# A chunk's token operands made from kept tokens inside the first unit, and the gate's iterations moved seven steps on

## The chip, the cores and the metric

One Trainium2 chip, one core. The metric is the device time of one execution, in microseconds; of repeated runs the median is given.

## The reference

Linear attention by random features, then a mixture of experts over all 2304 tokens (4 batches of 576, 8 heads of 64, so 512 columns; 8 experts of 1024 hidden columns). All inputs and outputs are float32.

```python
q_p, k_p = phi(q_s), phi(k_s)            # exp(x@omega.T - |x|^2/2 - max) / sqrt(128)
num = einsum('bhsm,bhmd->bhsd', q_p, einsum('bhsm,bhsd->bhmd', k_p, v))
den = einsum('bhsm,bhm->bhs', q_p, sum(k_p, 2)) + 1e-6
x = (num / den) as [2304, 512]
P = exp(x @ w_gate - max)                # [2304, 8]
for _ in range(8):
    P /= P.sum(1, keepdims=True) + 1e-9
    P /= P.sum(0, keepdims=True) + 1e-9
    P *= N / E
out = sum over e of P[:, e:e+1] * (maximum(x @ w1[e], 0) @ w2[e])
```

## The kernel before

**The attention** (`tick`, about 0 to 152 us) makes the tokens `x` in tiles of 128. Per tick PE makes the projections `pp`, the transpositions `tp`, `qp` of queries, the numerators `np`, and for a finished token tile its transposition `xp`; DVE takes maxima, shifts and quotients (`rd`, `xt`), ACT the exponentials `ex`. ACT's `token_copy` (L597) then puts the transposed tile into `xf`, a chunk of six tiles (768 tokens); there are three chunks. The attention's instructions are pinned in the order in which the code writes them.

**Products in seven.** Each matrix product of the experts is done in 2 by 2 blocks with seven products in place of eight, in the order 1, 5, 6, 3, 7, 2, 4, and each float32 operand as a rounded high part and a low rest, three products of parts. `token_operands` (L102) makes for a chunk its seven token operands: for four of them a total of quarters (L116, POOL, for the last chunk DVE), then the high part, called cast here (L120, ACT), the low (L124, DVE), and a store of both to a DRAM tile `xd` (L126, SP, 768 KB). A string (`plan`) says in which tick each is made. For the last chunk, chunk 2, the first products of the experts are interleaved with the making of its operands. `logits` (L168) makes a chunk's gate logits: products `lp` from `xf`, a copy `lg`, transpositions `gp`, and a sum into `prob`.

**The units.** There are 16, two for each expert (four blocks of 128 hidden columns each). A unit goes over the three chunks, the first one in the order 2, 0, 1, and has nine steps of two token tiles. `first` (L696) makes the products with w1 into the banks `hx` and `hz`; operands of the left side of the second product are made from them on DVE and ACT (`left_operands_a` and `_b`, L735 to L773); `second` (L796) makes the products with w2 into the banks `x` and `z`, which DVE adds to the outputs `out` (L818 in expert 0, with the factor of `prob` at L821 after it). Meanwhile ACT, DVE and POOL split the weights of the next unit (L250, L251, L217). `load_next` loads the next token operand from `xd` into one of four buffers `xs` each time one has been used.

**The gate.** `sinkhorn` (L610) is a generator of some 19 parts: maximum, exponential, and eight iterations of two parts each, with nine small DVE operations and one column product `cp` on PE in an iteration. The step loop takes two parts in each step (L1035), from the first step on. Expert 0 is added up without its factor; at its end, in unit 2, the loop writes a multiply of each output tile by its column of `prob` (L1015).

The units' instructions are put in order by a scheduler, so an instruction need not stand where the loop writes it.

Of the kernel before, what the change touches and what calls it, by code (L numbers as in the profile page):

```python
# [9 lines left out]
F32 = mybir.dt.float32  # L10
# [12 lines left out]
def moe_attention_kernel(  # L23
# [26 lines left out]
    N, DM = out.shape  # L50
    E = w_gate.shape[1]
    FF = w1.shape[2]
    P = 128
    KD = DM // P
# [9 lines left out]
    CT = 6  # L64
    NCH = NT // CT
    CL = CT * P
    HL = CL // 2
# [24 lines left out]
    ORDER = [1, 5, 6, 3, 7, 2, 4]  # L92
# [2 lines left out]

    W2AT = [(5, 2), (6, 0), (6, 3), (7, 0), (7, 3), (8, 0), (8, 3)]
    xdram = {}

    def token_tile():
        return xs.tile([P, 2, 2, HL], F32R, tag="xs", bufs=XSB, name="xs")  # L100

    def token_operands(c, x):  # L102

        def q(r, h):
            h = 1 - h
            return x[:, 2 * r : 2 * r + 2, h * HL : (h + 1) * HL]

        last = c == NCH - 1
        gate_steps = logits(c, x)
        if last:  # L110
            next(gate_steps)

        def total(o, i, s):
            eng = nc.vector if last else nc.gpsimd
            a, b = {5: (q(0, 1), s), 6: (q(1, 1), s), 7: (q(1, 1), q(0, 1)), 4: (q(1, 0), s)}[i]
            eng.tensor_tensor(o, a, b, op=ALU.subtract)  # L116

        def cast(i, o):
            t = token_tile()
            nc.scalar.copy(t[:, 0], o)  # L120
            return t

        def low(i, o, t):
            nc.vector.tensor_tensor(t[:, 1], o, raw(t[:, 0]), op=ALU.subtract)  # L124
            xdram[c, i] = xd.tile([P, 2, 2, HL], F32, name=f"xd{c}_{i}")
            nc.sync.dma_start(out=xdram[c, i], in_=raw(t))  # L126

        if last:
            for i in ORDER:
                n = len(traced)  # L130
                o = {3: q(1, 1), 7: q(0, 1), 2: q(1, 0)}.get(i, q(0, 0))
                if i in (5, 6, 7, 4):
                    total(o, i, o)
                t = cast(i, o)
                low(i, o, t)
                pinned.extend(traced[n:])
                xop[0, c, i] = t
                first(0, c, i, 0)
                first(0, c, i, 1)
                next(gate_steps, None)  # L140
                yield
            return


        if c == 0:
            at = {i: {3: q(1, 1), 7: q(0, 1), 2: q(1, 0)}.get(i, q(0, 0)) for i in ORDER}
            plan = "|c1 |c3 l1.s5|c2 l3|c5 l2.s7| l5.s6|c7 |c6 l7| l6.s4| |c4 | l4|"
        else:
            at = {1: q(0, 0), 3: q(1, 1), 2: q(1, 0)}
            for n, i in enumerate((5, 6, 7, 4)):  # L150
                at[i] = vts[n].rearrange("p h c -> p (h c)")[:, : 2 * HL].rearrange("p (k t) -> p k t", k=2)
            plan = "|s5.c1.c3 s7.l1|c2 l3.s6|c5 l2.s4|c7 l5|c6 l7|c4 l6.l4|"
        tiles = {}
        for n, step in enumerate(plan.split()):
            for part in step.split("|"):
                for what in part.split(".") if part else ():
                    i = int(what[1])
                    if what[0] == "s":
                        total(at[i], i, {5: q(0, 0), 6: at[5], 4: at[6]}.get(i))
                    elif what[0] == "c":  # L160
                        tiles[i] = cast(i, at[i])
                    else:
                        low(i, at[i], tiles.pop(i))
                yield
            next(gate_steps, None)
# [132 lines left out]
                yield  # L298


    sc_cm = tc.tile_pool(name="sc", bufs=1, reuse_waits="tile")
    sc = sc_cm.__enter__()
    rw_cm = tc.tile_pool(name="rw", bufs=1, side="right", reuse_waits="tile")
# [71 lines left out]
    xf = {}  # L375
# [207 lines left out]
    def token_transposes(xt, j, t):  # L583

        c = t // CT
        if c not in xf:
            xf[c] = sc.tile([P, KD, CL], F32, tag="xf", bufs=2, name="xf")
        xps = bank("xp")
        xj = xt[:, j].rearrange("p h d -> p (h d)")
        for kk in range(KD):  # L590
            nc.tensor.transpose(xps[:, kk * P : (kk + 1) * P], xj[:, kk * P : (kk + 1) * P], ident)
        return xps
# [50 lines left out]
    outt = {}  # L643
# [11 lines left out]
    def load_next():  # L655

        while loads:
            u, c, i = loads.pop(0)
            if i in RES:
                if (c, i) not in xres:  # L660
                    xres[c, i] = op_.tile([P, 2, 2, HL], F32R, name=f"xr{c}_{i}")
                    nc.sync.dma_start(out=raw(xres[c, i]), in_=xdram[c, i])
                xop[u, c, i] = xres[c, i]
                continue
            xop[u, c, i] = token_tile()
            nc.sync.dma_start(out=raw(xop[u, c, i]), in_=xdram[c, i])
            return
# [108 lines left out]
            6: (sh[:, 0], sl[:, 0]), 3: (sh[:, 1], sl[:, 1]), 2: (bh[:, 0], bl[:, 0]), 4: (bh[:, 1], bl[:, 1]),  # L776
        })

    acc = {}

    def second(s, i):


        u, n = steps[s]
        key, start = {1: ("x", 1), 6: ("x", 0), 7: ("x", 0), 4: ("x", 0), 5: ("z", 1), 3: ("z", 0), 2: ("z", 0)}[i]
        final = s == len(steps) - 1
        if final and i == 4:

            key, start = "y", 1
        if start:  # L790
            acc[key] = bank(key)
        pb = acc[key][:, HD:] if i in (5, 3) else acc[key][:, :HD]
        start = start or i == 2
        prods = [(a, b, f) for a, b in ((0, 0), (0, 1), (1, 0)) for f in range(2)]
        for j, (a, b, f) in enumerate(prods):
            nc.tensor.matmul(  # L796
                pb, lhsT=ops[s][i][a][:, f], rhs=wt[u, 2, i][b][:, f],
                start=bool(start) and j == 0, stop=j == len(prods) - 1, skip_group_check=True,
            )
        e, fb = units[u]  # L800
        r, col, init = {
            1: (0, 0, 1), 6: (0, 1, 1), 7: (1, 1, 0), 4: (1, 0, 1), 5: (1, 1, 1), 3: (0, 1, 0), 2: (0, 0, 0),
        }[i]
        if i == 3:
            return
        pair = tiles_of(u, n)
        t = pair[r]
        if u == 0 and i == 1:
            for tt in pair:
                outt[tt] = op_.tile([P, DM], F32, name=f"out{tt}")  # L810
        o = outt[t][:, col * HD : (col + 1) * HD]
        if i == 2:
            o, pb = outt[t], acc[key]
        if e == 0:
            if u == 0 and init:
                nc.scalar.copy(o, pb)
            else:
                nc.vector.tensor_tensor(o, pb, o, op=ALU.add)  # L818
            return
        p = prob[:, t, e : e + 1]  # L820
        nc.vector.scalar_tensor_tensor(o, in0=pb, scalar=p, in1=o, op0=ALU.mult, op1=ALU.add)  # L821
        if final and i == 7:
            o = outt[t][:, :HD]
            nc.vector.scalar_tensor_tensor(o, in0=pb, scalar=p, in1=o, op0=ALU.mult, op1=ALU.add)
# [185 lines left out]
    for s, (u, n) in enumerate(steps):  # L1010
        c = n // (CT // 2)
        more = u + 1 < len(units)
        if u == NFB:
            for t in tiles_of(u, n):
                nc.vector.tensor_scalar_mul(outt[t], outt[t], prob[:, t, 0:1])  # L1015
        if more:
            if n == 1:
                stage(u + 1, 1)
            if n == 2:
                split(u + 1, 1, ORDER[0])  # L1020
            if n == 2:
                stage(u + 1, 2)
        for k, i in enumerate(ORDER if s + 1 < len(steps) else [1, 5, 6, 3, 2, 4, 7]):
            second(s, i)
            if more and (n, k) in W2AT:
                split(u + 1, 2, ORDER[W2AT.index((n, k))])
            if k < ((5, 5, 4) if s > 2 else (3, 4, 3))[n % 3] and todo:
                pc = todo.pop(0)
                first(*pc)
                j = ORDER.index(pc[2])  # L1030
                if pc[1] == order(pc[0])[-1] and pc[3] == 1 and pc[0] + 1 < len(units) and j + 1 < len(ORDER):
                    split(pc[0] + 1, 1, ORDER[j + 1])
            if i == 7 and s + 1 < len(steps):
                left_operands_a(s + 1)
            if k in (1, 4):  # L1035
                next(gate, None)
        if s + 1 < len(steps):
            left_operands_b(s + 1)
        if s == NFB * NP - 1:
            for _ in gate:  # L1040
                pass
        if u == len(units) - 1:
            t0, t1 = tiles_of(u, n)
            for t, col in ((t0, 1), (t1, 1), (t0, 0), (t1, 0)):
                store(t, col, nc.scalar if s + 1 == len(steps) and t == t1 else nc.sync)
        ops.pop(s)
# [28 lines left out]
```

## Time and profile before

| | us |
|---|---|
| median of 3 runs | 1586.25 (1585.63 to 1586.45) |
| the profiled execution | 1585.57 |
| its span | 1583.8 |
| PE busy | 1561.0 (99%) |
| DVE busy | 1376.4 (87%) |
| ACT busy | 769.3 (49%) |
| POOL busy | 272.1 (17%) |

The profile is of one execution. Busy times are sums over the span; where an engine waited, and for whom, stands in the timelines (idle time in square brackets, with the one that ended it) and in the chain of waits.

### The profile page before, as it was taken

What the parts mean: (1) busy time and instruction counts of PE and PEld (TensorE: products, weight loads), DVE (VectorE), ACT (ScalarE), POOL (GpSimd) and SP (SyncE); (2) the same over time, 40 slices, a digit from 0 to 9 for tenths busy, and PEclk for the clock granted to TensorE, in tenths of its full rate; (3) what the DMA queues carried; (4) which work ended last, traced back from release to release, by engine and by line L of the source; (5) the groups of instructions that cost most, each with busy time, mean ns of one, the idle gap of its engine ahead of it and who ended that gap; (6) DMA issues with size and microseconds to landing.
All of it is one profiled execution on the core that took longest, in us unless ns stands there. A gap on an engine that the chain in (4) does not pass through costs nothing.

```text
span 1583.8 us, 31347 instructions
## 1 busy us (share of the span) xinstructions
PE 1561.0 (99%) x12337; PEld 1534.9 (97%) x12337; DVE 1376.4 (87%) x2600; ACT 769.3 (49%) x1393; POOL 272.1 (17%) x275
## 2 busy tenths in 40 slices
PE   8998999999999999999999999999999999999998
PEld 7876999999999999999999999999999999999997
DVE  6998998999889888889888888989888888888778
ACT  7987655444444444444444444443343444444332
POOL 4664211111011111102010111111010111110000
PEclk9999999999999999999999999999999999999999
DMA  9645866656656665656566666656566565645562
GB/s 220 144 148 219 341 233 215 226 176 242 216 206 218 226 206 202 224 189 227 202 214 212 218 217 208 222 183 224 194 226 226 207 207 208 239 166 182 198 220 80
DMA packets 105330, 329.79 MB, mean 208 GB/s; under 512 B 14816, under 2 KB 44000, under 8 KB 105184
## 3 DMA queue, kind: packets, MB, share of 16 engines
q1 hardware_dynamic: 104896, 327.53, 61.1%
q8 instruction: 98, 1.61, 0.4%
q14 instruction: 48, 0.39, 0.1%
q10 hardware_dynamic: 288, 0.26, 0.0%
HBM read 306.53 MB, written 21.23 MB: 207 GB/s over the span
## 4 chain that ended last, share of the span: by engine, by line
PE 89%; DVE 7%; ACT 2%; DMA 1%; issue 1%; POOL 1%; SPq 0%; DVEq 0%; ACTq 0%
PE hx L696 24%; PE x L796 24%; PE z L796 19%; PE hz L696 18%; DVE sqs L446 1%; DVE out L821 1%; PE pp L436 1%; DVE xs L124 1%; ACT ex L466 0%; PE np L556 0%; DVE wl L251 0%; DVE bl L735 0%; POOL sq L400 0%; PE qp L532 0%; DMA xs<-xd 0%
## 5 line engine op out<-in xcount | busy, mean ns | idle before, releaser
L696 PE MATMUL hx<-xs,wh 128*128 128x384 f32 x1536 | 369.0, 335 | 2.8 <-DMA xs<-xd 1.4
L821 DVE SCALAR_TENSOR_TENSOR out<-x,prob,out 128x256 f32<-128x256 f32 x503 | 236.0, 477 | 83.5 <-PE x L796 81.7
L696 PE MATMUL hz<-xs,wh 128*128 128x384 f32 x1152 | 285.0, 336 | 0.5 <-DVE bl L735 0.5
L696 PEld LDWEIGHTS hx<-xs,wh 128*128 128x128 f32 x1536 | 266.7, 188 | 4.3 <-ACT xs L120 2.0
L217 POOL TENSOR_TENSOR st<-st 128x512 f32<-128x512 f32 x75 | 120.9, 1612 | 616.6 <-DVE wl L251 612.5
L773 ACT ACTIVATE bh<-hr 128x512 fp32r<-128x512 f32 x144 | 91.1, 633 | 251.4 <-PE x L796 246.0
L696 PEld LDWEIGHTS hz<-xs,wh 128*128 128x128 f32 x1152 | 201.3, 188 | 1.6 <-DVE bl L735 1.1
L696 PE MATMUL hx<-xs,wl 128*128 128x384 f32 x768 | 200.6, 335 | 0.0
L821 DVE SCALAR_TENSOR_TENSOR out<-z,prob,out 128x256 f32<-128x256 f32 x252 | 153.3, 609 | 15.5 <-PE z L796 15.1
L250 ACT CAST wh<-st 128x512 fp32r<-128x512 f32 x172 | 103.4, 620 | 107.9 <-PE hx L696 53.9
L770 DVE TENSOR_TENSOR sl<-sm,sh 128x512 fp32r<-128x512 f32 x144 | 117.1, 813 | 41.5 <-ACT sh L769 33.9
L696 PE MATMUL hz<-xs,wl 128*128 128x384 f32 x576 | 152.5, 335 | 0.0
L769 ACT CAST sh<-sm 128x512 fp32r<-128x512 f32 x144 | 89.5, 621 | 102.7 <-PE z L796 80.2
L696 PEld LDWEIGHTS hx<-xs,wl 128*128 128x128 f32 x768 | 137.8, 188 | 0.0
L735 DVE SCALAR_TENSOR_TENSOR sm<-hr,sm 128x256 f32<-128x256 f32 x288 | 131.7, 457 | 3.2
L251 DVE TENSOR_TENSOR wl<-st,wh 128x512 fp32r<-128x512 f32 x172 | 123.2, 727 | 8.9 <-ACT wh L250 8.9
L756 ACT CAST sh<-sm 128x512 fp32r<-128x512 f32 x143 | 89.0, 622 | 67.7 <-PE x L796 64.6
L743 ACT ACTIVATE ah<-hr 128x256 fp32r<-128x256 f32 x144 | 60.2, 418 | 125.8 <-PE x L796 105.1
L796 PE MATMUL z<-wh,sh 128*128 128x256 f32 x576 | 119.0, 281 | 2.3 <-DVE out L821 1.3
L796 PE MATMUL x<-wl,sh 128*128 128x256 f32 x576 | 117.8, 280 | 0.0
L796 PE MATMUL z<-wl,sh 128*128 128x256 f32 x576 | 117.1, 280 | 0.0
L796 PE MATMUL x<-wh,sl 128*128 128x256 f32 x576 | 115.8, 279 | 0.2 <-DVE sl L770 0.2
(161 smaller groups left out, 3405.9 us busy)
## 6 DMA issues: line engine op xcount, KB each, us to landing
xs<-xd SPq DMA_DIRECT2D x329, 768.0 KB, 4.5
st<-in_moe_w_dram SPq DMA_DIRECT2D x64, 512.0 KB, 4.8
xd<-xs SPq DMA_DIRECT2D x21, 768.0 KB, 4.0
v<-in_v_dram SPq DMA_DIRECT2D x8, 512.0 KB, 6.9
q<-in_q_dram SPq DMA_DIRECT2D x8, 512.0 KB, 6.9
out_dram<-out SPq DMA_DIRECT2D x30, 128.0 KB, 2.0
k<-in_k_dram SPq DMA_DIRECT2D x7, 512.0 KB, 7.2
k<-in_k_dram SPq DMA_DIRECT2D x2, 256.0 KB, 3.0
```

What stands on the lines that cost most here:

```text
L217: nc.gpsimd.tensor_tensor(o, a, b, op=op)
L250: nc.scalar.copy(hi, o)
L251: nc.vector.tensor_tensor(lo, o, raw(hi), op=ALU.subtract)
L696: nc.tensor.matmul(pb, lhsT=a[:, k, g * P : (g + 1) * P], rhs=x[:, b, k, :], start=i in (1, 5, 2) and j == 0, stop=j == len(prods) - 1, sk ...
L735: nc.vector.scalar_tensor_tensor(o, in0=a, scalar=0.0, in1=b, op0=ALU.max, op1=op)
L743: nc.scalar.activation(ah, a11, AF.Relu)
L756: nc.scalar.copy(sh, sm)
L769: nc.scalar.copy(sh, sm)
L770: nc.vector.tensor_tensor(sl, sm, raw(sh), op=ALU.subtract)
L773: nc.scalar.activation(bh, a[:, 1:], AF.Relu)
L796: nc.tensor.matmul(pb, lhsT=ops[s][i][a][:, f], rhs=wt[u, 2, i][b][:, f], start=bool(start) and j == 0, stop=j == len(prods) - 1, skip_gro ...
L821: nc.vector.scalar_tensor_tensor(o, in0=pb, scalar=p, in1=o, op0=ALU.mult, op1=ALU.add)
```

## The change

For chunk 1 (`LATE`) no operand is made in the attention: of `token_operands` only its logits are left, and a function `make` that makes one operand (total on POOL, cast, low and store as before) is kept in `late`. `load_next` calls it in unit 0 where it loaded that operand before, so up to four products ahead of use. From unit 1 on, chunk 1's operands are loaded as before. The chunk's tokens stay in a buffer `xl` of its own; `xf` has one buffer in place of two. When `xl` is no longer read, the six output tiles of chunk 1 (`xo`) take its place. The gate's parts are taken from step 7 on.

```diff
--- before.py
+++ after.py
@@ -95,6 +95,8 @@
 
     W2AT = [(5, 2), (6, 0), (6, 3), (7, 0), (7, 3), (8, 0), (8, 3)]
     xdram = {}
+    LATE = NCH - 2
+    late = []
 
     def token_tile():
         return xs.tile([P, 2, 2, HL], F32R, tag="xs", bufs=XSB, name="xs")
@@ -142,14 +144,21 @@
             return
 
 
-        if c == 0:
-            at = {i: {3: q(1, 1), 7: q(0, 1), 2: q(1, 0)}.get(i, q(0, 0)) for i in ORDER}
-            plan = "|c1 |c3 l1.s5|c2 l3|c5 l2.s7| l5.s6|c7 |c6 l7| l6.s4| |c4 | l4|"
-        else:
-            at = {1: q(0, 0), 3: q(1, 1), 2: q(1, 0)}
-            for n, i in enumerate((5, 6, 7, 4)):
-                at[i] = vts[n].rearrange("p h c -> p (h c)")[:, : 2 * HL].rearrange("p (k t) -> p k t", k=2)
-            plan = "|s5.c1.c3 s7.l1|c2 l3.s6|c5 l2.s4|c7 l5|c6 l7|c4 l6.l4|"
+        at = {i: {3: q(1, 1), 7: q(0, 1), 2: q(1, 0)}.get(i, q(0, 0)) for i in ORDER}
+
+        if c == LATE:
+            def make(i):
+                if i in (5, 6, 7, 4):
+                    total(at[i], i, at[i])
+                t = cast(i, at[i])
+                low(i, at[i], t)
+                return t
+
+            late.append(make)
+            yield from gate_steps
+            return
+
+        plan = "|c1 |c3 l1.s5|c2 l3|c5 l2.s7| l5.s6|c7 |c6 l7| l6.s4| |c4 | l4|"
         tiles = {}
         for n, step in enumerate(plan.split()):
             for part in step.split("|"):
@@ -298,6 +307,7 @@
                 yield
 
 
+    xl = ctx.enter_context(tc.tile_pool(name="xl", bufs=1, reuse_waits="tile"))
     sc_cm = tc.tile_pool(name="sc", bufs=1, reuse_waits="tile")
     sc = sc_cm.__enter__()
     rw_cm = tc.tile_pool(name="rw", bufs=1, side="right", reuse_waits="tile")
@@ -584,7 +594,10 @@
 
         c = t // CT
         if c not in xf:
-            xf[c] = sc.tile([P, KD, CL], F32, tag="xf", bufs=2, name="xf")
+            if c == LATE:
+                xf[c] = xl.tile([P, KD, CL], F32, tag="xl", bufs=1, name="xl")
+            else:
+                xf[c] = sc.tile([P, KD, CL], F32, tag="xf", bufs=1, name="xf")
         xps = bank("xp")
         xj = xt[:, j].rearrange("p h d -> p (h d)")
         for kk in range(KD):
@@ -662,6 +675,9 @@
                     nc.sync.dma_start(out=raw(xres[c, i]), in_=xdram[c, i])
                 xop[u, c, i] = xres[c, i]
                 continue
+            if (u, c) == (0, LATE):
+                xop[u, c, i] = late[0](i)
+                return
             xop[u, c, i] = token_tile()
             nc.sync.dma_start(out=raw(xop[u, c, i]), in_=xdram[c, i])
             return
@@ -776,7 +792,7 @@
             6: (sh[:, 0], sl[:, 0]), 3: (sh[:, 1], sl[:, 1]), 2: (bh[:, 0], bl[:, 0]), 4: (bh[:, 1], bl[:, 1]),
         })
 
-    acc = {}
+    acc, late_out = {}, []
 
     def second(s, i):
 
@@ -807,7 +823,12 @@
         t = pair[r]
         if u == 0 and i == 1:
             for tt in pair:
-                outt[tt] = op_.tile([P, DM], F32, name=f"out{tt}")
+                if tt // CT == LATE:
+                    if tt == pair[0] and tt % CT == 0:
+                        late_out.append(xl.tile([P, CT, DM], F32, tag="xl", bufs=1, name="xo"))
+                    outt[tt] = late_out[0][:, tt % CT]
+                else:
+                    outt[tt] = op_.tile([P, DM], F32, name=f"out{tt}")
         o = outt[t][:, col * HD : (col + 1) * HD]
         if i == 2:
             o, pb = outt[t], acc[key]
@@ -1032,7 +1053,7 @@
                     split(pc[0] + 1, 1, ORDER[j + 1])
             if i == 7 and s + 1 < len(steps):
                 left_operands_a(s + 1)
-            if k in (1, 4):
+            if s > 6 and k in (1, 4):
                 next(gate, None)
         if s + 1 < len(steps):
             left_operands_b(s + 1)
```

In the changed kernel lines are numbered otherwise: L185 is `lp` (L176 before), L604 `xp` (L591), L566 `np` (L556), L126 the low (L124), L751 to L786 the left operands (L735 to L770), L839 the additions to `out` (L818), L1036 the multiply (L1015), L652 the last operation of a gate iteration (L639).

PE, where chunk 1's last token tiles are transposed, before:

```order
L532 MATMUL qp<-ident,ex 128x128 x8
L591 MATMUL xp<-ident,xt 128x128 x8
L556 MATMUL np<-kvs,qt 64x65 x16
L436 MATMUL pp<-omt,th 128x128 x8
L421 MATMUL tp<-ident,qr 128x128 x4
L532 MATMUL qp<-ident,ex 128x128 x8
L176 MATMUL lp<-xf,wgs 32x384 x8
```

and now:

```order
L542 MATMUL qp<-ident,ex 128x128 x8
L604 MATMUL xp<-ident,xt 128x128 x8
L185 MATMUL lp<-xl,wgs 32x384 x8
L566 MATMUL np<-kvs,qt 64x65 x16
L196 MATMUL gp<-ident,lg 128x128 x6
L446 MATMUL pp<-omt,th 128x128 x8
L431 MATMUL tp<-ident,qr 128x128 x4
L542 MATMUL qp<-ident,ex 128x128 x8
```

`lp`, chunk 1's logits, stands right behind the transpositions `xp`, and is followed by `np`; it stood behind `np`, `pp`, `tp` and `qp`.

DVE, multiplies of the outputs by `prob`, a stretch of the middle of unit 1 before:

```order
L818 TENSOR_TENSOR out_3655<-z,out_3655 128x512
L818 TENSOR_TENSOR out_3656<-x,out_3656 128x256
L770 TENSOR_TENSOR sl_4510<-sm,sh_4509 128x512
L1015 TENSOR_SCALAR out_3655<-out_3655,prob 128x512
L757 TENSOR_TENSOR sl<-sm,sh 128x512
L735 SCALAR_TENSOR_TENSOR sm<-hr,hn 128x512
L251 TENSOR_TENSOR wl<-t,wh 128x512
L735 SCALAR_TENSOR_TENSOR sm<-hr,sm 128x256 x2
L818 TENSOR_TENSOR out_3656<-x,out_3656 128x256
L735 SCALAR_TENSOR_TENSOR bl<-hr,bh 128x512
L1015 TENSOR_SCALAR out_3656<-out_3656,prob 128x512
```

and now, late in unit 1, where the last iteration of the gate ends:

```order
L652 TENSOR_TENSOR prob<-prob,ci 128x144
L1036 TENSOR_SCALAR out_3325<-out_3325,prob 128x512
L1036 TENSOR_SCALAR out_3326<-out_3326,prob 128x512
L1036 TENSOR_SCALAR out_3455<-out_3455,prob 128x512
L1036 TENSOR_SCALAR out_3456<-out_3456,prob 128x512
L1036 TENSOR_SCALAR out_3585<-out_3585,prob 128x512
L1036 TENSOR_SCALAR out_3586<-out_3586,prob 128x512
L1036 TENSOR_SCALAR xo<-xo,prob 128x512 x6
L1036 TENSOR_SCALAR out_3002<-out_3002,prob 128x512
L1036 TENSOR_SCALAR out_3003<-out_3003,prob 128x512
L786 TENSOR_TENSOR sl_5090<-sm,sh_5089 128x512
L839 TENSOR_TENSOR out_3101<-x,out_3101 128x256
```

The multiplies stood one by one between other work; 14 of the 18 now stand together behind the gate's last row (`xo` is the output of chunk 1).

DVE in unit 0, about 190 us in the trace of before:

```order
L818 TENSOR_TENSOR out_3142<-x,out_3142 128x256
L628 RECIPROCAL rs<-rs 128x18
L629 TENSOR_TENSOR prob<-prob,rs 128x144
L631 TENSOR_REDUCE cs<-prob 128x8
L713 TENSOR_TENSOR hr<-hz,hr 128x2x3x128
L251 TENSOR_TENSOR wl<-st,wh 128x512 x3
L818 TENSOR_TENSOR out_3141<-z,out_3141 128x512
L251 TENSOR_TENSOR wl<-st,wh 128x512
L770 TENSOR_TENSOR sl_3241<-sm,sh_3240 128x512
L713 TENSOR_TENSOR hr<-hx,hr 128x2x3x128
```

and now:

```order
L839 TENSOR_TENSOR out_3101<-x,out_3101 128x256
L729 TENSOR_TENSOR hr<-hz,hr 128x2x3x128
L260 TENSOR_TENSOR wl<-st,wh 128x512 x3
L839 TENSOR_TENSOR out_3100<-z,out_3100 128x512
L126 TENSOR_TENSOR xs<-xl,xs 128x768
L260 TENSOR_TENSOR wl<-st,wh 128x512
L786 TENSOR_TENSOR sl_3195<-sm,sh_3194 128x512
L260 TENSOR_TENSOR wl<-st,wh 128x512
L729 TENSOR_TENSOR hr<-hx,hr 128x2x3x128
L751 SCALAR_TENSOR_TENSOR bl<-hr,bh 128x512
L729 TENSOR_TENSOR hr<-hz,hr 128x2x3x128
L126 TENSOR_TENSOR xs<-xl,xs 128x768
```

The gate's rows (`rs`, `prob`, `cs`) are gone there, and lows (`xs<-xl,xs`) have come in.

## Rows read from the trace of the kernel before

**Rows 1.** The page, busy time and the span in 40 equal slices, in tenths.

```profile
PE 1561.0 (99%) x12337; PEld 1534.9 (97%) x12337; DVE 1376.4 (87%) x2600; ACT 769.3 (49%) x1393; POOL 272.1 (17%) x275
...
PE   8998999999999999999999999999999999999998
```

**Rows 2.** Windows: length, then each engine's busy us (instructions), PE clock, DMA share, GB/s.

```profile
130.00:140.00 10.00, 9.81 (x150) 8.06 (x144) 9.58 (x24) 8.91 (x22) 9.84 (x6) 1.00 0.30 120
190.00:200.00 10.00, 9.83 (x69) 9.63 (x69) 9.93 (x17) 5.08 (x11) 3.10 (x2) 1.00 0.63 205
280.00:320.00 40.00, 40.00 (x286) 40.00 (x285) 37.24 (x73) 18.49 (x30) 5.64 (x4) 1.00 0.68 227
```

**Rows 3.** PE timeline, 124 to 143 us: start, us, instruction [idle before <-releaser].

```profile
124.73 1.11 PE L591 MATMUL xp<-ident,xt 128*128 128x128 f32 x8
...
129.67 1.50 PE L176 MATMUL lp<-xf,wgs 128*32 128x384 f32 x16
...
136.64 1.15 PE L556 MATMUL np<-kvs,qt 128*64 128x65 f32 x32 [0.19 <-DVE ex L453]
...
141.35 1.10 PE L532 MATMUL qp<-ident,ex 128*128 128x128 f32 x4 [0.36 <-ACT ex L466]
142.65 0.66 PE L532 MATMUL qp<-ident,ex 128*128 128x128 f32 x4 [0.19 <-ACT ex L462]
```

**Rows 4.** ACT timeline, the token copies and one cast of chunk 1.

```profile
126.95 1.09 ACT L597 COPY xf<-xp 128x512 f32<-128x512 f32 x2
...
138.38 0.87 ACT L120 CAST xs<-v 128x768 fp32r<-128x768 f32 x1
```

**Rows 5.** DVE timeline, two lows and one late wait for PE.

```profile
136.83 1.41 DVE L124 TENSOR_TENSOR xs<-xf,xs 128x768 fp32r<-128x768 f32 x1
...
143.74 0.95 DVE L124 TENSOR_TENSOR xs<-v,xs 128x768 fp32r<-128x768 f32 x1
...
148.18 0.16 DVE L571 TENSOR_SCALAR rd<-np 128x4 f32<-128x4 f32 x1 [0.57 <-PE np L556]
```

**Rows 6.** PE timeline, chain of waits (start, us, what) and tile xd, at the handover.

```profile
171.87 0.59 PE L696 MATMUL hx<-xs,wh 128*128 128x384 f32 x2 [1.43 <-DMA xs<-xd]
...
160.22 4.92 DMA xd<-xs
...
165.22 6.51 DMA xs<-xd
...
DMA to landing us min/median/max: 3.2/4.5/13.6
```

**Rows 7.** Tile prob: operations with count, and ns as least/median/most.

```profile
L1015 DVE TENSOR_SCALAR out<-out,prob x18: 466/475/481, 282.7 to 362.7; 128x512 f32<-128x512 f32 x18
...
L631 DVE TENSOR_REDUCE cs<-prob x8: 416/442/452, 191.6 to 266.4; 128x8 f32<-128x144 f32 x8
L639 DVE TENSOR_TENSOR prob<-prob,ci x8: 286/307/309, 201.5 to 277.0; 128x144 f32<-128x144 f32 x8
```

**Rows 8.** POOL timeline, totals and weight sums; DVE timeline beside the latter.

```profile
128.12 3.67 POOL L116 TENSOR_TENSOR v<-xf 128x768 f32<-128x768 f32 x2 [3.45 <-ACT xf L597]
...
184.79 3.10 POOL L217 TENSOR_TENSOR st<-st 128x512 f32<-128x512 f32 x2 [1.29 <-DVE wl L251]
...
186.66 1.79 DVE L735 SCALAR_TENSOR_TENSOR bl<-hr,bh 128x512 fp32r<-128x512 f32 x1
```

**Rows 9.** DVE timeline of unit 2: two multiplies in a row.

```profile
340.42 0.87 DVE L1015 TENSOR_SCALAR out<-out,prob 128x512 f32<-128x512 f32 x2
```

**Rows 10.** Chain of waits, unit 0 and the last unit: start, us, what.

```profile
212.40 1.41 PE z L796 x12
...
225.94 2.08 PE hx L696 x12
...
1558.71 0.33 DVE al L735
...
1565.47 0.60 DVE bl L735
```

## Prediction

> **What bounds the kernel now.** I read the page first, for who is busy: PE has 1561.0 of 1583.8 us, and its slices fall below nine tenths only in the first and the last [rows 1]. The windows come next: PE is not quite full in the attention (9.81 of 10 us at 130 to 140) nor in unit 0 (9.83 at 190 to 200), and is exactly full in unit 1 (40.00 of 40), at a granted clock of 1.00 throughout [rows 2]. So only three things can move the end: the attention before 152 us, the handover to unit 0 (152 to 200), and any new idle time of PE behind it. Work taken off another engine is worth what PE waits for that engine, and no more. The second engine to watch is DVE: 9.93 of 10 us at 190 to 200 and 37.24 of 40 in unit 1 [rows 2]. The timelines of PE, ACT and DVE then give the single waits, and the chain of waits gives the one wait for a DMA.
>
> The sum is made against the profiled execution, 1585.57 us, which is 0.68 below the median of the runs (1586.25).
>
> **Attention: seven casts and seven lows leave, one group of PE products comes earlier: +0.7.** Removed are seven casts on ACT (0.87 each [rows 4]), seven lows on DVE (0.95, or 1.41 beside POOL's totals) [rows 5] and four totals on POOL (3.67 for two [rows 8]). What that is worth are PE's waits behind those engines. Three belong to it: 0.19 for DVE, 0.36 for ACT, 0.19 for ACT; and a group of four products that took 1.10 where the same shape takes 0.66, so 0.44 more [rows 3]. That makes 1.2; with a few tenths in shorter stretches I take 1.4. The last 8 us of the attention hold no more: there DVE waits for PE (0.57 at 148.18 [rows 5]), a chain from product to quotient to transposition to copy, which three lows fewer do not shorten.
>
> Against it stands a wait that the order of PE makes. The logits' products `lp` now stand right behind the transpositions `xp`, where `np`, `pp`, `tp` and `qp` stood between them. `lp` reads the kept tokens, whose two copies on ACT run to 126.95 + 1.09 = 128.04 [rows 4], while `xp` ends at 124.73 + 1.11 = 125.84 [rows 3]. Queued behind the waiting `lp` on PE are the tick's `np` and then `pp`, on which DVE's quotients and ACT's `ex` wait in turn. Before, `lp` waited for nothing (129.67, no idle time before it [rows 3]). So the wait is 2.2 us. The bounds: if all of it is made up later in the attention, only the gain of 1.4 remains; if nothing is gained, 2.2 is lost. I take both in full, 2.2 - 1.4 = +0.8, and since ACT has one cast less ahead of the copies I round to **+0.7**.
>
> **Handover: two stores leave the queue ahead of chunk 2's: -1.4.** PE waits 1.43 us at 171.87 for the load of a token operand [rows 6]. The chain shows what stands ahead of that: a store that lands after 4.92 us, then a load of 6.51; the fastest store lands in 3.2 [rows 6]. By the code, chunk 1's last stores are issued right before chunk 2's first, on the same queue, and they go. The store in the chain then comes nearer to 3.2, 1.7 us sooner, and the whole 1.43 goes. The bounds are 0 (the load alone is late) and **-1.4**; I take the latter, since 1.7 covers 1.43.
>
> **Unit 0: seven loads become seven operands made on the spot: +0.2.** Per operand: a cast (0.87 on ACT), a low (0.95 on DVE), a store of the same size in place of the load on SP's queue; and four totals on POOL. An operand is ready 1.8 us after its buffer is free, where a load took at least as long as the store's 3.2, so PE gets it no later. ACT is busy 5.08 of 10 us there and hides its casts [rows 2]. DVE, at 9.93, hides nothing: 7 x 0.95 = 6.7 us. But the gate leaves the same stretch. One of its iterations touches `prob` four times (0.44 for the longest, 0.31 for the multiply) and works five times on 8 or 18 numbers; 4 x 0.35 + 5 x 0.22 is 2.5 us, an estimate from these. Its eight multiplies by `ci` lie between 201.5 and 277.0, one per 10.8 us [rows 7], so some 2.5 iterations, 6.2 us, leave the 27 us in which the lows come. Net 0.5, of which I take **+0.2**; bounds 0 and +4.4 (below, C). That gate is done again in unit 1 where DVE has 2.8 us free in 40 [rows 2]; spread out, I price it at 0 there, and at half a us if PE catches one iteration late.
>
> **End of the gate: 14 multiplies in a row: +2.4.** Before, the gate ends at 277 and the 18 multiplies by `prob` lie one by one between 282.7 and 362.7 [rows 7], between other DVE work. Now the gate ends in the last steps of unit 1, the outputs of most steps of that unit are already waiting, and the order has 14 multiplies without anything between. On DVE, from the gate's last column product to the next read that PE waits for (`out_3220<-z`, which frees the bank `z`): the gate's tail, a multiply of 0.31 and three operations of about 0.21, 0.95; 14 multiplies at 0.40 (two in a row take 0.87 with the overhang [rows 9]), 5.6; then six rows of 512 at 0.60, five of 256 at 0.33 and one multiply [rows 10], 5.7. Together 12.2 us. In the same stretch PE has 24 products of 128x384 and 48 of 128x256, 2 x 2.08 + 4 x 1.41 = 9.8 us [rows 10]. PE waits for the rest, 2.4. Bounds: 0, if DVE is ahead when the gate ends or the bank is not needed at once, and 3.5, if DVE is a little behind. I take **+2.4**, the plain difference.
>
> Here one rule bears on unit 0. The trace has DVE slow beside POOL: while POOL does two sums in 3.10 us, one DVE row takes 1.79 [rows 8], where the same shape takes 0.60 [rows 10]. That is 1.2 for a POOL operation of 1.55, most of it but not all. The Trainium skill (SBUF — State Buffer, Who interferes with whom) says that a DVE instruction with two SBUF inputs contends with a GpSimd instruction that reads SBUF, and that the loser is blocked for the whole instruction. By that rule the four totals could cost DVE their full length, and the sum would end 7.3 us later than without them.
>
> **Sum:** 0.7 - 1.4 + 0.2 + 2.4 = +1.9. 1585.57 + 1.9 = 1587.5, and 1588.2 on the median's footing; I say **1588.0**. A measurement of this kernel can tell about 0.2%, 3.2 us, from no change; so "faster" is below 1583.1 and "slower" above 1589.4.
>
> **The rivals.**
>
> *A, both new waits are swallowed.* `lp`'s wait is made up in the latency chain of the attention's last 8 us, and the burst finds DVE ahead, as 2.8 us free in 40 allow [rows 2]. Then -1.4 and +0.2 are left: 1586.25 - 1.2 = 1585.0. No change. Against it: the wait on PE in the attention lies where PE has 9.81 of 10 us. Chance 0.15.
>
> *B, everything visible is gained and nothing lost.* 1.4 in the attention, 1.4 at the handover, and the short waits that PE still has in unit 0 (0.17 us in 10 [rows 2], so 0.8 in its 48). 1586.25 - 3.6 = 1582.6. Against it: it needs the 2.2 of `lp` not to happen at all. Chance 0.15.
>
> *C, POOL's totals take DVE's time in unit 0.* The place is steps 2 to 4 of unit 0. Four totals of 1.83 [rows 8], each stretching DVE by some 1.1, make 4.4 us more of DVE work in a stretch where it has 0.07 of 10 us free [rows 2]; from the point at which DVE's rows are later than PE's next bank, PE waits for all of it. 1588.0 + 4.2 = 1592.2. Against it: the same stretching stands in the trace of before, and PE lost 0.17 us in 10 there [rows 2]. Chance 0.20. The full block, with 4 x 1.83 = 7.3 in place of 4.4, gives 1595.1, chance 0.05; the row with 1.2 of 1.55 speaks for the smaller.
>
> **How the numbers follow.** Forecast 0.45 (own range 1585 to 1590.5: mostly inside the 0.2%, 0.07 above), A 0.15, B 0.15, C 0.25. Faster is B, 0.15; slower is C and the forecast's edge, 0.32; the same 0.53. The range runs from B's middle, about 1582.5, to a little above C's, 1593.0; outside are half of B and the full block with the upper part of C, together under 0.2.
>
> **What would show it.** In the changed profile: a wait of PE of about 2 us before `lp<-xl` at 126, released by ACT's copy; no wait for `xs<-xd` near 170; stores `xd<-xs` from 185 to 215 with lows beside; DVE full from 190 to 215 with PE above 9.7 of 10; 14 multiplies side by side near 340, and a wait of PE of about 2 us for an `out` row of DVE behind them. I am wrong if `lp` starts without a wait, if the burst leaves PE full, or if PE loses over 1 us in 185 to 215.

## The result and the profile after

The changed kernel takes 1603.62 us (median of 4 runs, 1603.36 to 1604.97) beside 1586.12 for the kernel before (1585.63 to 1586.45): a ratio of 1.0112, interval 1.01 to 1.0125. That is 17.5 us slower; the forecast was 1.9 us slower, its range ended at 1593.0. One slow execution, h1's profiled one (2027.88 us at a granted clock of 0.70), is left out of h1's median and of the table below.

The busy times of the page: DVE and ACT did the same work as before, PE's busy time rose by 6.4 us [rows 1], although the products are the same.

```profile
PE 1567.4 (98%) x12337; PEld 1540.9 (96%) x12337; DVE 1375.1 (86%) x2600; ACT 769.4 (48%) x1393; POOL 276.9 (17%) x275
```

The windows (as in [rows 2]: length, busy us of PE, PEld, DVE, ACT, POOL, then PE's granted clock, DMA share, GB/s) show where: in unit 0, and where unit 1 turns into unit 2. In three of them the granted clock is below 1; between the two places PE is full, as it was (280 to 320).

```profile
190.00:200.00 10.00, 8.53 (x60) 8.32 (x58) 9.35 (x12) 5.15 (x11) 5.63 (x4) 1.00 0.27 105
200.00:210.00 10.00, 7.67 (x41) 7.46 (x41) 7.88 (x10) 3.87 (x8) 4.01 (x2) 0.83 0.55 194
220.00:230.00 10.00, 7.45 (x42) 7.24 (x41) 6.38 (x11) 3.87 (x7) 4.31 (x3) 0.83 0.82 259
280.00:320.00 40.00, 40.00 (x290) 40.00 (x289) 38.49 (x94) 16.79 (x28) 5.89 (x4) 1.00 0.66 229
360.00:400.00 40.00, 36.17 (x238) 35.73 (x237) 35.31 (x69) 16.07 (x28) 7.59 (x4) 0.91 0.53 187
```

PE's timeline has the waits behind it. Against [rows 3]: from the last `qp` before the moved place to unit 0's first product, `hx`, 32.49 us pass now (120.97 to 153.46), where it was 31.54 (120.61 to 152.15). First the two rows of before, then those of now:

```profile
120.61 0.66 PE L532 MATMUL qp<-ident,ex 128*128 128x128 f32 x4 [0.19 <-ACT ex L462]
...
152.15 0.62 PE L696 MATMUL hx<-xs,wh 128*128 128x384 f32 x2
```

```profile
120.97 0.66 PE L542 MATMUL qp<-ident,ex 128*128 128x128 f32 x4 [0.19 <-ACT ex L472]
...
126.14 0.85 PE L185 MATMUL lp<-xl,wgs 128*32 128x384 f32 x8
128.46 0.85 PE L185 MATMUL lp<-xl,wgs 128*32 128x384 f32 x8 [1.47 <-ACT xl L610]
...
153.46 0.62 PE L712 MATMUL hx<-xs,wh 128*128 128x384 f32 x2
...
173.29 0.59 PE L712 MATMUL hx<-xs,wh 128*128 128x384 f32 x2 [1.51 <-DMA xs<-xd]
...
200.44 0.50 PE L812 MATMUL x<-wh,sl 128*128 128x256 f32 x2 [1.91 <-DVE sl L786]
...
203.54 0.84 PE L712 MATMUL hx<-xs,wh 128*128 128x384 f32 x2 [1.90 <-DVE hr L729]
...
224.24 1.01 PE L712 MATMUL hx<-xs,wh 128*128 128x384 f32 x2 [2.55 <-ACT hr L731]
...
369.17 0.80 PE L812 MATMUL z<-wh,sh 128*128 128x256 f32 x2 [3.74 <-DVE out L839]
...
373.17 0.84 PE L712 MATMUL hx<-xs,wh 128*128 128x384 f32 x2
```

At the handover the wait for the load is still there, 1.51 beside 1.43 [rows 6]. The chain (start, us, what) shows why: the store takes 0.6 us less than before to land and the load 0.7 more. Why the load takes longer stays open.

```profile
161.55 4.29 DMA xd<-xs
...
165.92 7.24 DMA xs<-xd
```

In unit 0, POOL's totals and DVE's rows beside them. Alone, the 128x512 row `sl` takes 0.6 to 0.7 us and a low 0.95 [rows 5]:

```profile
197.64 4.43 POOL L118 TENSOR_TENSOR xl<-xl 128x768 f32<-128x768 f32 x2 [2.10 <-DVE xs L126]
205.90 1.94 POOL L118 TENSOR_TENSOR xl<-xl 128x768 f32<-128x768 f32 x1 [3.83 <-DVE xs L126]
211.37 1.96 POOL L118 TENSOR_TENSOR xl<-xl 128x768 f32<-128x768 f32 x1 [3.53 <-DVE xs L126]
219.05 3.79 POOL L226 TENSOR_TENSOR t<-t,st 128x512 f32<-128x512 f32 x1 [5.71 <-DVE wl L260]
```

```profile
196.62 0.94 DVE L126 TENSOR_TENSOR xs<-xl,xs 128x768 fp32r<-128x768 f32 x1
...
198.09 2.30 DVE L786 TENSOR_TENSOR sl<-sm,sh 128x512 fp32r<-128x512 f32 x1
200.31 2.31 DVE L260 TENSOR_TENSOR wl<-st,wh 128x512 fp32r<-128x512 f32 x1
...
211.54 2.61 DVE L126 TENSOR_TENSOR xs<-xl,xs 128x768 fp32r<-128x768 f32 x1
...
219.23 0.95 DVE L126 TENSOR_TENSOR xs<-xl,xs 128x768 fp32r<-128x768 f32 x1
```

The rows that lie beside a total last 2.30, 2.31 and 2.61 us: each some 1.7 more than alone, nearly the total's whole length. The low at 211.54, for one, ends at 214.15, 0.8 us behind the total's end (211.37 + 1.96 = 213.33), about its own length. Only the total at 205.90 met an idle DVE. In turn the weight sum at 219.05 took POOL 3.79 us while DVE did four rows from 219.23 on, and PE's wait of 2.55 hangs on it through ACT's order: the copy of `hx` stands behind a cast that waits for that sum.

```profile
222.87 0.62 ACT L259 CAST wh<-t 128x512 fp32r<-128x512 f32 x1 [3.58 <-POOL t L226]
223.40 0.79 ACT L731 COPY hr<-hx 128x768 f32<-128x768 f32 x1
```

At the turn of unit 1 to unit 2, DVE's multiplies lie in a row, as the order said. From the first row behind the gate's last column product to the end of the read that PE waits for, 14.0 us pass (355.07 to 369.11) in place of the 12.2 forecast:

```profile
355.07 0.17 DVE L649 TENSOR_SCALAR ci<-cp 128x8 f32<-128x8 f32 x1
...
356.06 2.47 DVE L1036 TENSOR_SCALAR out<-out,prob 128x512 f32<-128x512 f32 x6
358.44 2.47 DVE L1036 TENSOR_SCALAR xo<-xo,prob 128x512 f32<-128x512 f32 x6
360.81 0.89 DVE L1036 TENSOR_SCALAR out<-out,prob 128x512 f32<-128x512 f32 x2
...
365.61 1.50 DVE L1036 TENSOR_SCALAR out<-out,prob 128x512 f32<-128x512 f32 x1
...
367.36 1.41 DVE L751 SCALAR_TENSOR_TENSOR bl<-hr,bh 128x512 fp32r<-128x512 f32 x1
368.70 0.41 DVE L839 TENSOR_TENSOR out<-z,out 128x256 f32<-128x256 f32 x1
```

Beside the last rows POOL has two weight sums, and DVE's rows of 0.40 and 0.60 become 1.50 and 1.41.

```profile
365.18 3.05 POOL L226 TENSOR_TENSOR st<-st 128x512 f32<-128x512 f32 x2 [45.71 <-DVE wl L260]
```

Last, the clock. The chain of waits has groups of 12 products of 128x384 right behind two of the waits, and the windows there have the granted clock (the third number from the end):

```profile
203.54 3.92 PE hx L712 x12
...
224.24 3.90 PE hx L712 x12
```

```profile
203.50:207.00 3.50, 3.46 (x11) 3.46 (x12) 2.66 (x4) 0.68 (x2) 1.10 (x1) 0.54 0.56 195
369.00:374.00 5.00, 4.83 (x21) 4.84 (x22) 4.11 (x11) 2.33 (x4) 1.40 (x1) 0.50 0.01 3
```

3.92 and 3.90 us in place of 2.08 [rows 10]: the lower of the clock's two levels, 1.2 in place of 2.4 GHz. Some 1.7 us are lost so behind each of the two waits: from the first of the 12 products to the start of the row behind them 3.76 and 3.74 us pass (to 207.30 and 227.98). Behind the wait of 3.74 the 18 products of 128x256 from 369.17 to 373.17 took 4.0 us in place of 2.1, and `hx` behind them was slow at first (0.84 for two), 2.5 us in all.

### The profile page after: what moved, and what is told of

Same layout as the page of the kernel before. It is cut to its first block, busy times and chain, and to the rows that moved or that the text cites. A ratio compares the mean times of both kernels' runs of the same rounds, so it can differ in the third digit from the quotient of the medians.

```text
span 1601.9 us, 31328 instructions
## 1 busy us (share of the span) xinstructions
PE 1567.4 (98%) x12337; PEld 1540.9 (96%) x12337; DVE 1375.1 (86%) x2600; ACT 769.4 (48%) x1393; POOL 276.9 (17%) x275
## 4 chain that ended last, share of the span: by engine, by line
PE 84%; DVE 3%; DMA 1%; issue 1%; POOL 0%; ACT 0%; DVEq 0%; SPq 0%
PE hx L712 24%; PE x L812 24%; PE z L812 18%; PE hz L712 18%; DVE wl L260 1%; DMA xs<-xd 0%; DVE out L842 0%; DVE sm L751 0%; DVE sl L786 0%; DVE out L1036 0%; DMA xd<-xs 0%; DVE xo L842 0%; POOL t L226 0%; DVE bl L751 0%; DVE sl L773 0%
## 5 line engine op out<-in xcount | busy, mean ns | idle before, releaser
L842 DVE SCALAR_TENSOR_TENSOR out<-x,prob,out 128x256 f32<-128x256 f32 x335 | 159.6, 479 | 56.8 <-PE x L812 54.8
L786 DVE TENSOR_TENSOR sl<-sm,sh 128x512 fp32r<-128x512 f32 x144 | 115.9, 805 | 44.5 <-ACT sh L785 38.8
L751 DVE SCALAR_TENSOR_TENSOR sm<-hr,sm 128x256 f32<-128x256 f32 x288 | 130.3, 452 | 3.0
L812 PE MATMUL x<-wh,sh 128*128 128x256 f32 x576 | 115.4, 280 | 0.9 <-DVE out L842 0.9
```

What stands on the lines that cost most here:

```text
L751: nc.vector.scalar_tensor_tensor(o, in0=a, scalar=0.0, in1=b, op0=ALU.max, op1=op)
L786: nc.vector.tensor_tensor(sl, sm, raw(sh), op=ALU.subtract)
L812: nc.tensor.matmul(pb, lhsT=ops[s][i][a][:, f], rhs=wt[u, 2, i][b][:, f], start=bool(start) and j == 0, stop=j == len(prods) - 1, skip_gro ...
```

## The experiments

To compare the runs, I take from each trace when each product of the experts starts, less the time that all products before it take at the full rate (2.08 us for 12 of 128x384, 1.41 for 12 of 128x256 [rows 10]); what this difference grows by in a stretch is what PE lost there. "Unit 0" is from 20 to 150 us of products (unit 0, first part of unit 1), "the turn" from 150 to 240 (the rest of unit 1, most of unit 2), "rest" from 240 to 1400. The stretches are those of the one profiled execution of each run, which lay up to 2.2 us from the median (e4 1596.77, h2 1592.36, g2 1592.20; g0 1586.03). What comes before unit 0 differs between executions: in the six kernels with the attention of before, its first product starts between 151.75 and 154.05 us.

| run | median us | unit 0 | turn | rest |
|---|---|---|---|---|
| before | 1585.7 to 1586.1 | 3.4 | 0.2 | 4.4 |
| the change | 1603.62 | 12.3 | 8.9 | 4.7 |
| e1, totals on DVE | 1601.48 | 3.7 | 13.6 | 4.9 |
| e2, no totals | 1599.19 | 4.1 | 9.8 | 5.4 |
| e3, gate early | 1599.80 | 14.7 | 0.7 | 5.6 |
| e5, logits later | 1603.66 | 12.8 | 9.5 | 4.1 |
| f7, no totals, gate early | 1591.44 | 7.1 | 0.4 | 6.4 |
| f1, totals on DVE, gate early, logits later | 1593.34 | 10.6 | 0.8 | 3.9 |
| h3, multiplies spread | 1603.56 | 12.0 | 5.9 | 6.9 |
| g1, totals on DVE, logits later, multiplies spread | 1592.90 | 3.8 | 5.5 | 6.0 |
| g3, as g1, the gate four steps on | 1592.88 | 6.3 | 3.0 | 6.4 |
| h2, three late operands, gate early | 1590.25 | 8.8 | 0.1 | 5.9 |
| e4, before with the late gate | 1594.59 | 2.5 | 10.4 | 4.2 |
| g2, before with the gate four steps on | 1590.21 | 3.7 | 5.8 | 4.7 |
| f3, before, late gate, no multiplies | 1587.06 | 2.5 | 2.0 | 4.4 |
| g0, before, late gate, multiplies spread | 1587.11 | 2.3 | 2.8 | 3.5 |
| k1, before, chunk 1's outputs in one tile | 1586.16 | 3.4 | 0.2 | 4.2 |

The theories: a POOL total holds a DVE operation for its length (H) against the mere amount of DVE work (Q); and the multiplies in a row (B).

**Is it POOL's totals?** e1 puts them on DVE, e2 leaves them out, with the gate still late.

```diff
-            eng = nc.vector if last else nc.gpsimd
+            eng = nc.vector if last or c == LATE else nc.gpsimd
```

```diff
-                if i in (5, 6, 7, 4):
-                    total(at[i], i, at[i])
```

> The change with the four totals of the late operands made on DVE in place of POOL. Theory H (a POOL total holds a DVE operation for its whole length): DVE gets 4 x 0.95 = 3.8 us more work but loses three holds of about 1.7 us each, and PE's waits at 198 to 204 us of the changed kernel (1.91 and 1.90, then 12 products at half the clock, together 5.5) fall by more than half: 1597 to 1600 us. Theory Q (it is the amount of DVE work in unit 0, seven lows, that makes PE wait, POOL is no matter): 3.8 us more of it makes it worse, 1605 to 1609 us.

> The change without the four totals of the late operands (left out: the operands of products 5, 6, 7 and 4 of chunk 1 are then plain quarters of the tokens). Theory H: with no POOL total beside DVE the waits at 198 to 204 us and their half clock go (5.5 us), what stays is the wait of 2.6 us behind ACT's copy and the one in unit 2: 1595 to 1599 us. Theory Q: lows and casts are all still there, so PE waits as long: 1602 to 1604 us.

Measured: 1601.48 and 1599.19, so by time alone H looks half right. By stretch it is right: unit 0 loses 3.7 and 4.1 in place of 12.3, as little as before the change. PE's timeline of e1, with the waits for the load, for `sl` and for `hr`:

```profile
173.65 0.58 PE L712 MATMUL hx<-xs,wh 128*128 128x384 f32 x2 [2.39 <-DMA xs<-xd]
...
199.00 0.50 PE L812 MATMUL x<-wh,sl 128*128 128x256 f32 x2 [0.30 <-DVE sl L786]
...
200.47 0.62 PE L712 MATMUL hx<-xs,wh 128*128 128x384 f32 x2 [0.26 <-DVE hr L729]
```

The waits of 1.91 and 1.90 are 0.30 and 0.26 (that for the load, ahead of the stretch, is 2.39 in place of 1.51). So the lows, and even four totals more on DVE, are covered there once POOL is out of it. But e1 then lost 13.6 at the turn: expecting the rest of the time to stay as it was is what failed in both expectations. Why e1 loses more there than the change's 8.9 stays open.

**Is it the burst of multiplies?** e3 has the change with the gate as before, e4 the kernel before with the late gate alone, f3 that without the multiplies, g0 that with the multiplies held apart.

```diff
-            if s > 6 and k in (1, 4):
+            if k in (1, 4):
```

```diff
                 nc.vector.tensor_scalar_mul(outt[t], outt[t], prob[:, t, 0:1])
+                tc.add_manual_dep(traced[-1], ends[s - 2], in_order, reason="multiplies stay near their step")
...
         ops.pop(s)
+        ends[s] = next(x.name for x in reversed(traced) if x.engine == mybir.EngineType.DVE)
```

> The change with the gate's iterations where they were before (from the first step on). Theory B (the 14 multiplies in a row cost PE its wait of 3.7 us in unit 2 and 2.4 us of half clock behind it): that wait goes, 6.1 us; unit 0 gets 2.5 iterations, 6 us of DVE work, back. If unit 0 then loses no more than now, 1597 us; if all 6 us come back as PE's wait, 1603 us. A rival by which the wait in unit 2 comes from something else (weight sums on POOL) has it stay at 3 us or more.

> The kernel before with nothing but the gate moved seven steps on. Theory B: a wait of PE of 2 to 4 us for DVE's out in unit 2, with half clock behind it if it is longer than about 2 us: 1589 to 1593 us, and no waits in unit 0. Rival (the burst of multiplies is hidden, and it is the late operands that make DVE late up to there): 1586 us.

> The kernel before with the gate seven steps on, and without the 18 multiplies of the outputs by prob (left out: expert 0's share then has no factor). Theory B (the multiplies, which then come in a row, cost PE its wait): no wait in unit 2, 1585 to 1587 us. Rival (the gate's iterations at the end of unit 1, with two parts per step where DVE has its left operands to make, are what makes DVE late): 1590 to 1594 us.

> The kernel before with the gate seven steps on, and each multiply of an output held by an order on DVE behind the step two before its own, so that they lie in pairs over the nine steps of unit 2. Theory B (it is that they stand in a row): 8 us of the late gate's 9 go, 1586 to 1588.5 us, no wait of PE over 1 us in unit 2. Rival (the multiplies cost their time wherever they stand once the gate is late): 1591 to 1594 us.

Measured: e3 1599.80, e4 1594.59, f3 1587.06, g0 1587.11 (ratio 1.0007, interval 0.9998 to 1.0017). The late gate alone costs the kernel before 8.9 us (1594.59 beside 1585.71), more than I expected, with one wait in PE's timeline of e4:

```profile
361.51 0.80 PE L796 MATMUL z<-wh,sh 128*128 128x256 f32 x2 [5.66 <-DVE out L818]
```

Without the multiplies, or with the same multiplies in pairs over nine steps, all but about 1 us of it goes. So the row of multiplies is shown to be the cause, not the late iterations nor the amount of work. Part of the row's price is again POOL: in e4 its first ten multiplies took 6.12 us in place of 4.1, beside two weight sums that ran from 352.90 to 355.81. g0's window at the same place has PE full:

```profile
340.00:380.00 40.00, 40.00 (x283) 39.85 (x282) 36.12 (x75) 17.61 (x30) 5.40 (x4) 1.00 0.65 224
```

In e3 the turn is free (0.7), but the gate's iterations are back in unit 0 beside lows and totals, and PE waits there again, the longest times for 1.50, 1.48 and 2.09 us:

```profile
214.60 0.50 PE L812 MATMUL z<-wh,sl 128*128 128x256 f32 x2 [1.50 <-DVE sl L773]
...
234.97 0.61 PE L712 MATMUL hz<-xs,wh 128*128 128x384 f32 x2 [2.09 <-DVE hr L729]
```

g2 asks how far the gate can be moved in the kernel before: four steps in place of seven.

> The kernel before with the gate four steps on in place of seven. Ten multiplies then stand nearly together in the order, a few steps sooner. Theory B with PE's lead over DVE as the measure: 4 x 0.4 us less DVE work in the row than with seven steps and other work between: 1587 to 1591 us. A rival by which the late end of the gate counts, and not the row, has half of seven steps' loss: 1590 us with the loss spread over unit 1.

Measured: 1590.21, between the kernel before and e4, and the loss lies at the turn (5.8), not in unit 0. The rival by the late end had the same time, so the time alone does not decide here. The place speaks for the row: the longest wait, 1.82 us at 327.23, is for an ACT copy that waits for DVE's `bl`, and `bl` stands behind the first three multiplies (324.47).

**What do the early logits cost?** e5 has the change with chunk 1's logits two parts of a tick later, as before.

```diff
-            yield from gate_steps
-            return
+            for _ in range(2):
+                yield
+                yield
+                next(gate_steps, None)
+            return
```

> The change with chunk 1's logits where they were before (two parts later). The wait of 1.5 us before them in the attention goes; the rest stays. Theory: unit 0 begins 0.9 us sooner against the last query products, 1602.3 to 1603 us. Rival (the attention's end is a chain that swallows it): 1603.6 us, with the first product of unit 0 no sooner.

Measured: 1603.66 beside 1603.62, no change in time. Yet in PE's timeline unit 0 begins 1.8 us sooner after the same `qp` than in the change, 30.70 us (32.49; before 31.54). This stretch is the same to 0.04 us in all traces with the same attention, six of before's, six of the change's and four of e5's:

```profile
120.88 0.66 PE L545 MATMUL qp<-ident,ex 128*128 128x128 f32 x4 [0.19 <-ACT ex L475]
...
151.58 0.61 PE L715 MATMUL hx<-xs,wh 128*128 128x384 f32 x2
```

So removing the casts and lows shortens the attention by 0.84 us, and the early `lp` costs 1.8. e5's time cannot show it: with four runs each the intervals reach 2 to 3 us to either side (1.0096 to 1.013 for e5). In the profiled executions I can only place, not explain, where it goes: of its lead of 1.9 us over the change, 0.5 goes in unit 0, 0.6 at the turn and 0.9 behind the last products, and 0.6 comes back in the rest, so that the profiled spans differ by 0.5 (1601.4 beside 1601.9).

**Does the move pay with its faults put right?** f1 has totals on DVE, the early gate and the later logits; f7 no totals and the early gate; g1 totals on DVE, later logits, spread multiplies, and the late gate; g3 is g1 with the gate four steps on.

> The change with three parts put right at once: totals on DVE, gate from the first step, chunk 1's logits two parts of a tick later, as before the change. If the losses are what the runs so far say (burst of multiplies 8 to 11 us, POOL totals in unit 0 9 us, early logits 0.9 us), all three go and what stays is the seven lows and four totals on DVE beside the gate in unit 0, 10 us of DVE work where it has little free: 1588 to 1592 us. If the late operands cost nothing once POOL is out, 1585 to 1586 us.

> The change without the four totals (left out) and with the gate from the first step: what is left against the kernel before is that seven casts and seven lows are made in unit 0. Theory H: with POOL out of it the lows cost little: 1587 to 1590 us. Theory Q: 6.7 us more of DVE work beside the gate make PE wait for most of it: 1592 to 1596 us.

> The change with totals on DVE, logits two parts later, and the multiplies spread over unit 2 as in the run before this one. Attention 0.8 us shorter than before, unit 0 with eleven DVE operations more and no gate beside them 1 to 3 us longer, the gate in unit 1 beside the weights' splits 1 us, no burst: 1586 to 1589.5 us. If it falls under 1585.5 the idea of the change pays; over 1591 and DVE's work in unit 0 is a loss by itself, gate or no gate.

> As the second run of these, with the gate four steps on in place of seven: one iteration and a half more in unit 0's last steps, the same spread multiplies. If the gate's DVE work in unit 1 costs, it is better than with seven steps by up to 1 us; if unit 0 is the tight place, it is worse by 1 to 2 us: 1586 to 1591 us.

Measured: 1593.34, 1591.44, 1592.90 and 1592.88. None of the four comes near the kernel before, and no run was faster than it. With the gate early, unit 0 loses 7.1 without totals, 10.6 with them on DVE and 14.7 with them on POOL, beside 3.4: so beside the gate seven lows cost 3.7 even without totals, as theory Q has it. With the gate late unit 0 is free, and the turn is not.

Three runs asked what is left. h1 is g1 with no totals at all, h2 makes only the three operands late that need no total (gate early), h3 is the change with spread multiplies alone; k1 is the kernel before with chunk 1's outputs in one tile, as the change has them.

```diff
-            if (u, c) == (0, LATE):
+            if (u, c) == (0, LATE) and i in (1, 3, 2):
```

> The change with logits two parts later, multiplies spread over unit 2, and the four totals left out (the operands of products 5, 6, 7 and 4 of chunk 1 are plain quarters). Theory A (what is left is the amount of DVE work moved out of the attention): 3.8 us less of it than with totals on DVE, so 3 to 4 us faster than that, 1588.5 to 1590.5 us. Rival (the many short waits come from the late gate or from chunk 1's outputs in one tile): no change, 1592 to 1594 us.

> Only the three operands of chunk 1 that need no total (products 1, 3, 2) are made late; the other four in the attention as before, the gate from the first step. Theory A: DVE gets 2.9 us in unit 0 beside the gate, of which PE waits for half to all, and the attention gives back 0.2 to 0.5: 1586.5 to 1588.5 us. If it is under 1585.5, a small move pays where the large one does not.

> The change with nothing but the multiplies spread over unit 2. Theory B: the wait of 3.7 us in unit 2 with its half clock goes, 6 to 8 us: 1595.5 to 1598 us; the waits of unit 0 (with half clock, 9 us) stay. Rival (DVE is late there anyway, the loss moves on): 1600 us or more.

> The kernel before with nothing but chunk 1's six outputs in one tile in place of six. If the common tile costs (an instruction on one output waits for another engine's instruction on its neighbour), 1588 to 1592 us, with the loss at the end of unit 0 and in unit 1. If not, 1585.3 to 1586.7 us, and the rest of the loss is in the late operands themselves.

Measured: h1 1593.13, h2 1590.25, h3 1603.56, k1 1586.16 (ratio 1.0002, interval 0.9992 to 1.0012). h1 refutes theory A: 3.8 us less of DVE work than in g1 gains nothing. k1 rules out the common tile, and that it takes the place of `xl` costs the change no wait: the last read of `xl` ends at 221.7 us, the first write of `xo` is at 246.4. h2 loses 4.3 us with only three lows, most of it at one place, where DVE's rows lie beside POOL's weight sums:

```profile
211.67 1.42 POOL L226 TENSOR_TENSOR t<-t,st 128x512 f32<-128x512 f32 x1 [16.49 <-DVE wl L260]
...
221.87 1.61 POOL L226 TENSOR_TENSOR st<-st 128x512 f32<-128x512 f32 x1
```

```profile
211.91 1.99 DVE L126 TENSOR_TENSOR xs<-xl,xs 128x768 fp32r<-128x768 f32 x1
...
215.30 1.52 DVE L751 SCALAR_TENSOR_TENSOR al<-hr,ah 128x256 fp32r<-128x256 f32 x1
...
220.93 1.40 DVE L773 TENSOR_TENSOR sl<-sm,sh 128x512 fp32r<-128x512 f32 x1
222.26 1.77 DVE L751 SCALAR_TENSOR_TENSOR sm<-hr,hn 128x512 f32<-128x512 f32 x1
```

A low of 0.95 takes 1.99, three rows of the units' own work take 1.52, 1.40 and 1.77 in place of 0.4, 0.7 and 0.7, and at their end PE waits 1.35 us for `hr`, with the lower clock behind it. So the wait cannot be put down to the low alone. Nor does the number of lows order the runs: f7, with seven of them beside the same gate and no totals, loses 7.1 in unit 0, h2 8.8.

```profile
224.95 0.69 PE L712 MATMUL hx<-xs,wh 128*128 128x384 f32 x2 [1.35 <-DVE hr L729]
225.44 0.84 PE L712 MATMUL hx<-xs,wl 128*128 128x384 f32 x2
```

h3 takes away the wait of 3.74 and 3 us of the turn's 8.9, but its time stays: a wait of 1.98 for ACT's `hr` comes in its place (the copy waits for DVE's `bl`, which takes 1.76 beside two weight sums), and the rest of the run loses 2 us more. So in the change the multiplies are no term of their own: another row is late when they are gone. What makes up the 5.5 us that g1 loses at the turn, against 2.8 in g0, stays open.

## Why the prediction was wrong, by its steps

**Attention, +0.7: right in size.** It came to +0.95 (32.49 beside 31.54). Its two terms were both too large, and that the sum fits is luck: the early `lp` cost 1.8 in place of 2.2 (its wait was 1.47, because its first eight products read the chunk's first three tiles and ran at once, at 126.14), and what the lows give back was 0.84 in place of 1.4 (e5).

**Handover, -1.4: wrong.** I took the queue to be the cause, and the store to come nearer its fastest landing. It did by 0.6 us, but the load behind it took 0.7 longer, and the wait was 1.51 in place of 1.43. What I had as the lower bound, 0 for "the load alone is late", was the case.

**Unit 0, +0.2: the step that failed most.** It cost 8.9 us (12.3 beside 3.4), and its own sign of being wrong came: PE lost 1.5 us in 190 to 200 alone. Rival C named the place, steps 2 to 4, and the mechanism. But I argued that the same stretching in the trace before had cost PE little, and so gave it a chance of 0.25 and 4.4 us. Two things were left out of its price. PE's wait does not end with DVE: the late weight sum held ACT's copy of `hx`, 2.55 us more. And behind the waits of 1.90 and 2.55 a dozen products ran at half rate, 1.7 us lost each time. The amount of DVE work I had priced rightly: with the gate late, lows and casts are covered (e1, e2). On the size of a hold, the row with 1.2 of 1.55 spoke for the smaller value, and the three rows of 1.7 now speak for nearly the whole. The Trainium skill (SBUF — State Buffer, Who interferes with whom) has the loser blocked for the whole instruction; with holds of 1.7 beside totals of 1.9 to 2.2 the trace agrees.

**The row of multiplies, +2.4: right mechanism, wrong size.** It stands behind the gate's end, in the order's own form (at 356 us, where I had said near 340), and PE waits for the row that I named. The terms: DVE took 14.0 us in place of 12.2, since POOL's weight sums held two of its rows; the wait is 3.74 in place of 2.4; and 2.5 us of low clock follow. At the turn the change loses 8.7 us more than before, 6.2 of it here and the rest in shorter stretches.

**The range.** It was added up from waits alone, at the clock that all rows of before show. The lower clock behind three long waits makes some 5.9 us (1.7, 1.7 and 2.5), a third of the loss, and none of it could be read from [rows 2], where the clock stands at 1.00. C's 1592.2 already held both, the totals and the row of multiplies, and both happened; its sizes were 4.4 for 8.9 and 2.4 for 8.7.

## What to carry to other kernels

Ask of a small job moved to an idle engine beside a full one which rows will lie beside it, and price each as held for nearly the job's whole length; then follow the late row through the order of the other engines' work to the next product. When a late value releases many small operations at once, they stand in a row unless something holds them apart; if they are not needed at once, spread them. Where the matrix engine is otherwise never idle, price a new wait at its length and leave room in the range for the clock: in the change 1.7 to 2.5 us came on top at three places, and behind other waits nothing.

## What the runs showed of the hardware

DVE and POOL held each other for nearly a whole operation: DVE rows of 0.6 to 0.95 us lasted 2.30 to 2.61 beside totals of about 2 us, a DVE multiply of 0.40 lasted 1.50 beside a weight sum, and a weight sum that takes 1.3 us elsewhere took 3.79 beside four DVE rows.

PE's granted clock was 0.54 in the 3.5 us behind waits of 1.91 and 1.90 that lie close together, 0.54 behind one of 2.55, and 0.50 behind one of 3.74; 12 products then took 3.9 us in place of 2.08. In h2 it was 0.57 behind a wait of 1.35 (0.84 for the two products at 225.44). But behind a single wait of 1.51 it stayed at 1.00, in e1 behind one of 2.39 (0.58 for the next two products in the row at 173.65, as in [rows 6] behind 1.43), and in e3 behind 1.50, 1.48 and 2.09. So the length of a single wait did not decide it in these runs, and the bound of about 2 us in the expectation of e4 does not hold.
